# Two chained attentions and a max-of-three feed-forward layer: a new written order for the first two batches, an engine chosen for each copy, and a few idle products

## The chip, the cores and the metric

One core of a Trainium2 chip. The metric is the time of one execution in microseconds as the device measures it. The kernel before took 503.29 us (median of 3 runs, 502.99 to 503.62).

## The reference

Eight batches of 576 rows, eight heads of 64 columns. Keys and values are first packed by 32 learned rows `p`; the queries then attend to the 32 packed rows, which are keys and values at once. The heads side by side (4608 rows x 512) go through a feed-forward layer whose hidden value is the largest of three products.

```
p_packed = sm_attn(p, k, v)                 # softmax(p k^T / 8) v, per batch and head
out      = sm_attn(q, p_packed, p_packed)
x        = out, heads side by side          # 4608 x 512
h        = max(x @ w1, x @ w2, x @ w3)      # 4608 x 768
result   = h @ w_out                        # 4608 x 512
```

## The kernel before

The unit of work is a step: a Python generator that issues a few instructions and yields. Its name is a letter and digits, the first digit being the batch b (0 to 7). The heads of a batch are kept in two groups r = 0, 1, and the 576 rows in two halves of 288.

- `S` scores of `p` against the keys (L209); `A` the largest value, the exponential and the turn by TensorE (L222 to L256), per r; `Z` the inverse of the sum; `V` products with the values (L268); `K` the turn of the packed rows and their copy to `pt` (L283, L285).
- `Q` products of the queries with `pt` (L295), in two halves for batch 0. `B` the softmax over 32 columns, per r, for batch 0 also per half: turn (L318), maximum (L322), subtraction (L324), exponential (L326), sum (L329), inverse (L331, L333), multiplication (L335), turn (L338), and the split into a rounded high part `a2h` and a remainder `a2l` (L122, L127).
- `P` projects: as `x` is a combination of packed rows, each of the six column blocks j of the hidden layer needs `pt` times the weights (L356), scaled and split into `ph` (L365, ScalarE) and `pl` (L367, VectorE).
- `N` the hidden layer (L389), in groups of 6 products of 128x288 (high by high, low by high, high by low, for two r), called mi here; `E` the maximum of three (L399, L403, L405); `H` its split.
- `O` the output product (L434, called mo), `F` its copy and store.
- `C` converts weights, which are stored as 64-bit words: two ScalarE steps (L173, L178), one of VectorE (L184), one of GpSimd (L188). Each j takes three transfers `wi`. `k`, `v`, `q`, `w` are loads, all on SP's queue.

For batches 2 to 7 a table of due times (`STAGES`) and `tick` set the order on TensorE, and the scheduler that of the other engines. For batches 0 and 1, the conversion of all weights and the first part of batch 2, the order on every engine is written by hand: the table `START`, one word per advance of a step. A word ending in v, g or a sends what the advance issues to VectorE, GpSimd or ScalarE, where `on` or `split_hi` asks. Each engine works through its own queue in order.

Buffers that matter: two large PSUM tiles (tag `big`) serve the scores, the turned scores of batches above 0 and the projections; four PSUM banks (tag `moe`) serve the sums of N and O; `ph` and `pl` have three buffers each; q two; four tiles of `stage` hold weights on arrival; SP's loads are written in the order of `START`, and at most eight are under way, since each waits for the landing of the one eight before it.

Of the kernel before, what the change touches and what calls it, by code (L numbers as in the profile page):

```python
# [51 lines left out]
B011 A10 C11 N00 C12 N00 B001v E000 A11 B011g C11 E000 A11 E000 N00 C20 P01 Z11 C20 Z10 A10 P01 N00 w31
C22 A10 P01 C22 N00 A11 E001 C21 N01 E001 C21 A11 E001 N01 E010 C31 V101 w32 C30 q10 E010 C30 C31 q11
w40 H00a N01 V101 w41 H00g K1 P02 E010 K1 C32 C31 N01 P02 C31 N01 P02 E011 C32 N01 w42 E011 Q1 C32 E011
C32 H01a N02 B11 C40 w50 H01g N02 C40 B11 N02 E020 B10 B11g C41 N02 C41 B10 P10 B11 B10v E021 N02 B11
B10 P11 E020 B11 P10 B11 B10 B11g N02 C42 E020 B10 P11 B10 B11 B10g C42 P10 B11 B10 P03 C50 B11g E021
B10 E021 P03 B10v C50 P11 N10 H02a C42 N10 E100 C40 N10 P03 C42 N10 E100 C40 E100 N10 E101 N10 E101 w51
H02g N11 E101 H10a N11 C41 E110 C50 N11 E110 C41 N11 C51 E110 N11 C51 w52 C50 w60 E111 N11 w61 E111 w62
H10g N03 w63 E111 H11a N03 C51 E030 N03 C52 C51 E030 P04 E030 C52 H11g C60 N03 P04 N03 E031 P04 N03 C61
E031 N04 C61 E031 C60 N04 C52 C61 E040 N04 C52 C63 E040 N04 C62 E040 C60 C63 P12 C61 E041 C62 N04 P12  # L60
C60 N04 E041 C61a P12 P05 w64 C60a w65 C61v N12 H03a E041 C60g P05 N12 H04a P05 N12 H03g C64 N12 C64 P13
C63 E120 C62 E121 E120 C62 N12 C65 E120 P13 N12 E121 k20 C63 C65 P13 N05 C62a N05 E121 k21 C63a H04v N05
H12a C63v N05 E050 C62v N05 E051 E050 H12g N05 E050 E051 N13 C65 E051 C65 N13 E130 H05a N13 E130 C65a
H05v N13 E130 C65g N13 E131 N13 C64 O0 E131 C64 E131 O0 H13a O0 v20 C64v v21 C64v O0 q20 q21 H13g O0 O0
F00 O0 F01 O0 O0 O0 F02 O0 O0 O0 F03 O0 O0 O0 F04 O0 O0 P14 F05 O0 P14 O0 P14 O0 O0 F06 O0 O0 N14 F07
N14 E140 N14 E140 P15 E140 N14 P15 N14 P15 E141 N14 E141 N15 E141 H14a N15 E150 H14v N15 E150 N15 E150
# [14 lines left out]
def fused_kernel(ctx: ExitStack, tc: tile.TileContext, kp, qt, va, vb, wi, wo, out):  # L81
# [80 lines left out]
    def convert(j, c):  # L162

        words = staged.pop((j, c)).bitcast(U32).rearrange("p (n two) -> p n two", two=2)
        low, high = words[:, :, 0], words[:, :, 1]
        nc.scalar.activation(  # L173
            out=high.bitcast(F32), in_=high.bitcast(F32), func=AF.Prelu, scale=2.0 ** -111, alpha=-2.0 ** 32,
        )
# [66 lines left out]
    def turn(b, r):  # L242
# [6 lines left out]
        a = a1[b, r][0]  # L249
        for t in range(SF):  # L250
            nc.tensor.transpose(out=tp[:, t * P:(t + 1) * P], in_=a[:, t * P:(t + 1) * P], identity=ident)  # L251
# [4 lines left out]
        nc.scalar.copy(out=at[0:SR, SF, :], in_=pa[0:SR, 0:P])  # L256
# [23 lines left out]
    def packed(b):  # L280

        pt = av.pop((b, 1))[:, 2 * P:3 * P]
        nc.tensor.transpose(out=pt, in_=pp.pop(b).rearrange("p r d -> p (r d)"), identity=ident)  # L283
        yield 1
        nc.scalar.copy(out=pt_sb[b % 2], in_=pt)  # L285
# [64 lines left out]
    def project(b, j):  # L350

        ps = ps_big.tile([P, R, 512], F32, name=f"pw{b}_{j}", tag="big")
        for n in range(4):
            for r in range(R):
                o = slice(64 * r, 64 * r + 64)
                nc.tensor.matmul(  # L356
                    out=ps[NP * n:NP * n + NP, r, 0:NW * P],
                    lhsT=pt_sb[b % 2][o, NP * n:NP * n + NP],
# [6 lines left out]
        nc.scalar.activation(out=hi, in_=ps[:, :, 0:NW * P], func=AF.Copy, scale=2.0 ** -WS)  # L365
        yield 1
        nc.vector.scalar_tensor_tensor(  # L367
            out=lo, in0=ps[:, :, 0:NW * P], scalar=2.0 ** -WS, in1=hi.bitcast(F32), op0=ALU.mult, op1=ALU.subtract,
        )
# [88 lines left out]
    def keep_warm(n):
        t = ps_moe.tile([P, 512], F32, name="idle", tag="moe")
        for _ in range(n):  # L460
            nc.tensor.matmul(out=t[:, 0:P], lhsT=ident, rhs=ident, start=True, stop=True)

# [146 lines left out]
```

## Time and profile before

| | |
|---|---|
| time, median of 3 runs | 503.29 us |
| the profiled execution: time, span | 503.85 us, 502.1 us |
| TensorE busy | 479.2 us, 95% of the span |
| VectorE, ScalarE, GpSimd busy | 237.1, 209.6, 129.5 us |
| mean granted clock of TensorE | 0.983 |
| mean traffic with memory | 102 GB/s of the span |

The span runs from the first to the last instruction; 1.75 us of the time lie outside it. A row of the timeline gives start and duration in us, the engine, the line of the kernel, the tile written and those read, and in brackets the idle time ahead and what ended it. Durations of neighbouring rows overlap by some 0.1 us, as instructions are pipelined: the distance between two starts says what one costs in a full queue.

### The profile page before, as it was taken

How to read it: one execution, taken by the hardware profiler on the slowest of the kernel's cores; microseconds unless marked ns; L12 is line 12 of the kernel's file. 1: busy time of each engine (PE TensorE's matmuls, PEld its weight loads, DVE VectorE, ACT ScalarE, POOL GpSimd, SP SyncE). 2: the span in 40 equal slices, each digit the busy share in tenths (PEclk: the TensorE clock that was granted, in tenths of full speed). 3: DMA queues.
4: the chain of work that ended last, by engine and by line, in shares of the span. 5: the costliest groups of instructions: out<-in, count | busy, mean ns of one | idle time of the engine just before them, and what ended most of it. 6: DMA issues, size and time to landing. Idle time of an engine off the chain costs nothing.

```text
span 502.1 us, 11442 instructions
## 1 busy us (share of the span) xinstructions
PE 479.2 (95%) x4888; PEld 425.9 (85%) x4888; DVE 237.1 (47%) x483; ACT 209.6 (42%) x437; POOL 129.5 (26%) x104
## 2 busy tenths in 40 slices
PE   4569899999999999999999999999999999999997
PEld 2238698998997989988899899989899898999997
DVE  1595947812436548054551537235470536524410
ACT  3776859412325534244342434335341443433321
POOL 0377576510002223212240222201241122302200
PEclk9679899999999999999999999999999999999999
DMA  8957272451262322130321222112331000110001
GB/s 298 407 206 277 70 252 86 153 189 49 89 207 96 106 95 95 72 112 19 116 99 72 106 88 103 48 49 105 95 119 48 25 3 1 47 48 1 1 25 71
DMA packets 17250, 52.11 MB, mean 104 GB/s; under 512 B 1968, under 2 KB 4272, under 8 KB 17200
## 3 DMA queue, kind: packets, MB, share of 16 engines
q1 hardware_dynamic: 17200, 51.39, 29.0%
q8 instruction: 38, 0.62, 0.5%
q14 instruction: 12, 0.10, 0.1%
HBM read 41.94 MB, written 9.44 MB: 102 GB/s over the span
## 4 chain that ended last, share of the span: by engine, by line
PE 87%; DMA 7%; ACT 1%; DVE 1%; POOL 1%; issue 1%; SPq 1%; ACTq 0%; DVEq 0%; POOLq 0%
PE mi L389 44%; PE mo L434 31%; PE pw L356 6%; DMA wi<-in_wi 4%; DMA v<-in_va 2%; PE tp L268 2%; DMA q<-in_qt 2%; PE s L295 1%; PE s L209 1%; PE tp L251 1%; POOL w_sb L188 1%; ACT wi L173 0%; DVE wo_lo L127 0%; PE tp L252 0%; SPq L151 0%
## 5 line engine op out<-in xcount | busy, mean ns | idle before, releaser
L389 PE MATMUL mi<-a2h,ph 128*128 128x288 f32 x576 | 176.6, 307 | 3.6 <-ACT ph L365 2.4
L389 PE MATMUL mi<-a2h,pl 128*128 128x288 f32 x576 | 170.7, 296 | 1.6 <-DVE pl L367 1.6
L389 PE MATMUL mi<-a2l,ph 128*128 128x288 f32 x576 | 170.8, 297 | 0.4 <-POOL a2l L127 0.4
L434 PE MATMUL mo<-h,wo_hi 128*128 128x288 f32 x768 | 156.6, 297 | 0.0
L389 PEld LDWEIGHTS mi<-a2h,ph 128*128 128x128 f32 x576 | 108.8, 189 | 29.1 <-issue 15.4
L434 PEld LDWEIGHTS mo<-h,wo_hi 128*128 128x128 f32 x768 | 124.3, 188 | 2.3 <-issue 1.6
L434 PE MATMUL mo<-h,wo_lo 128*128 128x288 f32 x384 | 113.8, 296 | 0.0
L127 POOL TENSOR_TENSOR h<-hf,h 128x576 fp32r<-128x576 f32 x38 | 54.5, 1435 | 221.5 <-ACT h L122 221.5
L389 PEld LDWEIGHTS mi<-a2h,pl 128*128 128x128 f32 x576 | 109.0, 189 | 1.9 <-DVE pl L367 1.9
L389 PEld LDWEIGHTS mi<-a2l,ph 128*128 128x128 f32 x576 | 108.8, 189 | 0.9 <-POOL a2l L127 0.6
L367 DVE SCALAR_TENSOR_TENSOR pl<-pw,ph 128x768 fp32r<-128x768 f32 x48 | 44.7, 952 | 109.3 <-ACT ph L365 109.3
L399 ACT COPY c<-mi 128x288 f32<-128x288 f32 x96 | 38.2, 398 | 82.6 <-PE mi L389 81.8
L434 PEld LDWEIGHTS mo<-h,wo_lo 128*128 128x128 f32 x384 | 72.3, 188 | 0.2 <-DVE wo_lo L127 0.2
L403 DVE TENSOR_TENSOR c<-mi,c 128x288 f32<-128x288 f32 x96 | 43.5, 453 | 60.8 <-PE mi L389 60.0
L447 ACT ACTIVATE o<-mo 128x288 f32<-128x288 f32 x64 | 26.2, 411 | 99.3 <-PE mo L434 95.1
L405 DVE TENSOR_TENSOR hf<-mi,c 128x288 f32<-128x288 f32 x96 | 43.8, 456 | 25.3 <-PE mi L389 22.5
L122 ACT CAST h<-hf 128x576 fp32r<-128x576 f32 x48 | 32.3, 673 | 48.0 <-DVE hf L405 47.3
L356 PE MATMUL pw<-w_sb,pt 64*32 64x384 f32 x768 | 40.1, 503 | 4.8 <-DVE e L318 2.1
L365 ACT ACTIVATE ph<-pw 128x768 fp32r<-128x768 f32 x48 | 37.0, 808 | 15.1 <-PE pw L356 15.0
L324 POOL TENSOR_TENSOR e<-e,m 128x576 f32<-128x576 f32 (+1 forms) x15 | 15.7, 1063 | 60.6 <-PE mo L434 45.8
L188 POOL TENSOR_TENSOR w_sb<-w_sb,wi 128x512 int32<-128x512 int32 x18 | 24.4, 1364 | 25.1 <-DMA wi<-in_wi 14.8
L356 PEld LDWEIGHTS pw<-w_sb,pt 64*32 64x32 f32 x768 | 11.1, 106 | 17.1 <-issue 13.1
(64 smaller groups left out, 329.5 us busy)
## 6 DMA issues: line engine op xcount, KB each, us to landing
kt<-in_kp SPq DMA_DIRECT2D x16, 640.0 KB, 5.1
wi<-in_wi SPq DMA_DIRECT2D x18, 512.0 KB, 8.5
out_t<-o SPq DMA_DIRECT2D x31, 288.0 KB, 2.1
v<-in_va SPq DMA_DIRECT2D x16, 512.0 KB, 4.5
q<-in_qt SPq DMA_DIRECT2D x14, 576.0 KB, 5.2
wo<-in_wo SPq DMA_DIRECT2D x6, 512.0 KB, 6.8
q<-in_qt SPq DMA_DIRECT2D x4, 288.0 KB, 8.0
v<-in_vb SPq DMA_DIRECT2D x16, 64.0 KB, 4.7
```

The costliest lines, as they stand in the source:

```text
L122: e.copy(out=hi, in_=src)
L127: on(default).tensor_tensor(out=lo, in0=src, in1=hi.bitcast(F32), op=ALU.subtract)
L188: nc.gpsimd.tensor_tensor(out=dst.bitcast(I32), in0=dst.bitcast(I32), in1=up, op=ALU.add)
L356: nc.tensor.matmul(out=ps[NP * n:NP * n + NP, r, 0:NW * P], lhsT=pt_sb[b % 2][o, NP * n:NP * n + NP], rhs=w_sb[o, j, n * NW * P:(n + 1) * ...
L365: nc.scalar.activation(out=hi, in_=ps[:, :, 0:NW * P], func=AF.Copy, scale=2.0 ** -WS)
L367: nc.vector.scalar_tensor_tensor(out=lo, in0=ps[:, :, 0:NW * P], scalar=2.0 ** -WS, in1=hi.bitcast(F32), op0=ALU.mult, op1=ALU.subtract,)
L389: nc.tensor.matmul(out=sums[b, j, hf, x][:, 0:HS], lhsT=w[:, r, x * P:(x + 1) * P], rhs=a[:, c], start=(r == 0 and n == 0), stop=(r == R - ...
L399: nc.scalar.copy(out=c1, in_=sums[b, j, hf, 0][:, 0:HS])
L403: nc.vector.tensor_tensor(out=c1, in0=sums[b, j, hf, 1][:, 0:HS], in1=c1, op=ALU.max)
L405: nc.vector.tensor_tensor(out=hidden[b, j][:, c], in0=sums[b, j, hf, 2][:, 0:HS], in1=c1, op=ALU.max)
L434: nc.tensor.matmul(out=sums[b, m, hf][:, 0:HS], lhsT=w[:, j, x], rhs=a[:, c], start=(j == 0 and i == 0), stop=(j == NJ - 1 and i == 2),)
L447: nc.scalar.activation(out=o[:, c], in_=sums.pop((b, m, hf))[:, 0:HS], func=AF.Copy, scale=2.0 ** -WS)
```

## The change

`START` is written anew: 575 words in place of 568. The set of steps is the same, but for five words `I`, and for two advances more of step `P00`. With it:

- `copy` takes the place of `split_hi`, and now serves the copies of the turned scores (L255, L256), of `pt` (L285) and of the first of three sums (L399) too, so that a word's ending moves them to VectorE; the addition of 1e-9 (L331) and the output copy (L447) can go there as well.
- `I` no longer issues products at once: it sets a count, and the next step of `S`, `A`, `Q`, `P` or `N` that begins issues as many products of the identity with itself into its own PSUM tile first (`rouse`). The count is the word's first digit: `I10` gives one. In all there are seven: one ahead of S0, of the first turn, of Q0 and of P00, and three ahead of the first mi.
- `P00` writes two of the four `moe` banks, one per r, and splits them apart; before it took a `big` tile and did both at once.

The table itself shows nothing to a reader; its first two lines before and now are:

```diff
-k00 k01 v00 v01 w00 q000 q010 w01 w02 q001 q011 w10 w11 w12 S0 w20 w21 w22 k10 A00 k11 w30 A01 A00 A01
-A00 Z00 C00 Z01 A01 A00 A01 V00 C01 V01 V00 C01 v10 C02 V01 C01 v11 K0 C02 C01 K0 C00 Q0 C02 Q0 C00 B000
+k00 k01 I10 S0 w11 C11 C11 v01 w00 w02 v00 A01 A00 w01 A01 A00 q010 I10 A01 A00 A01v Z00 Z01 C11 A00v
+C00 C02 C00 C00 C02 C01 V01 C11 C00 q000 V00 V00 V01 K0 q001 q011 C01 w12 C02 C01 K0a I1 Q0 B000 Q0 B010
...
+    def copy(out, src, default="a"):
         e = on(default)
         if e is nc.scalar:
-            e.copy(out=hi, in_=src)
-        else:
-            e.tensor_copy(out=hi, in_=src)
+            e.copy(out=out, in_=src)
+        else:
+            e.tensor_copy(out=out, in_=src)
...
+    idle = [0]
+
+    def rouse(ps):
+
+        for _ in range(idle[0]):
+            nc.tensor.matmul(out=ps[:, 0:P], lhsT=ident, rhs=ident, start=True, stop=True)
+        idle[0] = 0
...
     def project(b, j):
 
-        ps = ps_big.tile([P, R, 512], F32, name=f"pw{b}_{j}", tag="big")
+        parts = [slice(0, R)]
+        if b == 0 and j == 0:
+
+            parts = [slice(r, r + 1) for r in range(R)]
+            ps = [ps_moe.tile([P, 512], F32, name=f"pw{b}_{j}_{r}", tag="moe") for r in range(R)]
+            src = [x[:, 0:NW * P].unsqueeze(1) for x in ps]
+        else:
+            x = ps_big.tile([P, R, 512], F32, name=f"pw{b}_{j}", tag="big")
+            ps, src = [x[:, r] for r in range(R)], [x[:, :, 0:NW * P]]
+        rouse(ps[0])
...
             if kind == "I":
-                keep_warm(x[0])
+                idle[0] = x[0]
```

SP's queue at the program's start. `wi0_1` is the second transfer of the weights of j = 0, `v1` the values of head group 1 of batch 0 (a transfer of 4 KB rows and a small one), `kt` keys, `q` half of the queries. Before:

```order
L144 DMA kt0_81<-in_kp 128x1280
L144 DMA kt1_83<-in_kp 128x1280
L150 DMA v0_85<-in_va 128x1024
L151 DMA v0_85<-in_vb 64x256
L150 DMA v1_88<-in_va 128x1024
L151 DMA v1_88<-in_vb 64x256
L138 DMA wi0_0_91<-in_wi 128x512
L159 DMA q0_93<-in_qt 128x2x288
L159 DMA q1_95<-in_qt 128x2x288
L138 DMA wi0_1_97<-in_wi 128x512
```

Now:

```order
L154 DMA kt0_81<-in_kp 128x1280
L154 DMA kt1_83<-in_kp 128x1280
L148 DMA wi1_1_104<-in_wi 128x512
L160 DMA v1_108<-in_va 128x1024
L161 DMA v1_108<-in_vb 64x256
L148 DMA wi0_0_111<-in_wi 128x512
L148 DMA wi0_2_113<-in_wi 128x512
L160 DMA v0_115<-in_va 128x1024
L161 DMA v0_115<-in_vb 64x256
L148 DMA wi0_1_126<-in_wi 128x512
```

Three transfers of weights, one of them for j = 1, moved ahead of the second part of the values; the queries now follow the tenth load.

VectorE's queue from the first turn of batch 0's scores on. `s2_0_0` is the PSUM tile of r = 0, `s2_0_1` that of r = 1, `m2` maxima, `z2` sums; each turn takes one half of 288. Before:

```order
L318 STREAM_TRANSPOSE e0_0_258<-s2_0_0_238 128x288
L322 TENSOR_REDUCE m2_0_0_0_262<-e0_0_258 128x9
L324 TENSOR_TENSOR e0_0_258<-e0_0_258,m2_0_0_0_262 128x288
L318 STREAM_TRANSPOSE e0_0_258<-s2_0_0_238 128x288
L318 STREAM_TRANSPOSE e0_1_270<-s2_0_1_239 128x288
L329 TENSOR_REDUCE z2_0_0_0_273<-e0_0_258 128x9
L322 TENSOR_REDUCE m2_0_1_0_275<-e0_1_270 128x9
L333 RECIPROCAL z2_0_0_0_273<-z2_0_0_0_273 128x9
L335 TENSOR_TENSOR e0_0_258<-e0_0_258,z2_0_0_0_273 128x288
L338 STREAM_TRANSPOSE et0_0_293<-e0_0_258 128x288
```

Now:

```order
L331 STREAM_TRANSPOSE e0_0_237<-s2_0_0_226 128x288
L331 STREAM_TRANSPOSE e0_1_247<-s2_0_1_227 128x288
L335 TENSOR_REDUCE m2_0_1_0_249<-e0_1_247 128x9
L335 TENSOR_REDUCE m2_0_0_0_251<-e0_0_237 128x9
L331 STREAM_TRANSPOSE e0_0_237<-s2_0_0_226 128x288
L331 STREAM_TRANSPOSE e0_1_247<-s2_0_1_227 128x288
L335 TENSOR_REDUCE m2_0_0_288_261<-e0_0_237 128x9
L335 TENSOR_REDUCE m2_0_1_288_265<-e0_1_247 128x9
L337 TENSOR_TENSOR e0_0_237<-e0_0_237,m2_0_0_288_261 128x288
```

All four turns and maxima now stand ahead of the first sum. The first turn is written between the two halves of Q0, and the second half of Q0 waits for it, as both touch the same tile. Nine more instructions stand between this piece and the turn `et0_0` of the first half.

TensorE's queue around the projection P03. `pw0_3` is its result, `pw1_1` that of batch 1's second, `mi0_2_1_2` the third sum of the second half of batch 0's j = 2. Before:

```order
L389 MATMUL mi0_2_1_1_696<-a2l0_1_376,ph0_2_587 128x288
L356 MATMUL pw1_1_706<-w_sb_72,pt1_76 32x384 x8
L389 MATMUL mi0_2_1_2_725<-a2h0_0_297,ph0_2_587 128x288
L389 MATMUL mi0_2_1_2_725<-a2h0_0_297,pl0_2_588 128x288
L389 MATMUL mi0_2_1_2_725<-a2l0_0_304,ph0_2_587 128x288
L389 MATMUL mi0_2_1_2_725<-a2h0_1_374,ph0_2_587 128x288
L389 MATMUL mi0_2_1_2_725<-a2h0_1_374,pl0_2_588 128x288
L389 MATMUL mi0_2_1_2_725<-a2l0_1_376,ph0_2_587 128x288
L356 MATMUL pw0_3_748<-w_sb_72,pt0_75 32x384 x8
L389 MATMUL mi1_0_0_0_771<-a2h1_0_761,ph1_0_718 128x288
```

Now:

```order
L417 MATMUL mi0_2_1_0_693<-a2h0_1_370,pl0_2_634 128x288
L417 MATMUL mi0_2_1_0_693<-a2l0_1_373,ph0_2_633 128x288
L381 MATMUL pw0_3_709<-w_sb_72,pt0_75 32x384 x8
L381 MATMUL pw1_1_737<-w_sb_72,pt1_76 32x384 x8
L417 MATMUL mi0_2_1_1_747<-a2h0_0_336,ph0_2_633 128x288
L417 MATMUL mi0_2_1_1_747<-a2h0_0_336,pl0_2_634 128x288
```

Before, P10, P11 and P03 stand with 6 mi between each two, and batch 1's mi begin behind P03. Now P02 and P10 stand together, 36 mi follow, then P03 and P11 together, then 48 mi more of batch 0 ahead of batch 1's first. Two more moves are told of below: batch 1's scores S1 stand ahead of the first mi and no longer behind 6 of them, and P01 stands behind 6 mi and no longer behind 24. From batch 2's first mi on, the instructions of TensorE stand as before.

More of the change, by code (lines that the diff above doesn't have):

```diff
@@ L52 @@
[L52 to L66, printed above, removed]
@@ new lines @@
+B010 B000 B001 C02 C01 B000g B010g C12 B011 C12 B001 B000 B010 B011 B001v k11 C12 w10 k10 B001 I1 P00
+B000 P00 B010 B000a B011g B001 B011 B010a C12 w22 P00 B000 B010 B000v B001a B001 C10 C10 B000 S1 w21
+B010g B001v C10 B000a B000g B001 B011 P00 C22 B011a A10 B010 A10 B001a I3 N00 C10 B011 B010v B011v B010g
+P01 P00 B011 C21 N00 P01 A11 A11 C22 N00 B011v A10 P01 A11 E000v w31 v11 v10 w20 E000 C21 C31 B001g E000
+B011g C22 A11v A10a N00 N00 V101 C31 C20 C20 N00 C22 C21 Z11 Z10 V101 C21 q11 K1 C20 E001v N01 q10 w30
@@ new lines @@
+K1a Q1 E001 E001 w32 C20 H00v C31 N01 H00g E010a B10 C31 N01 C30 w42 N01 P02 w41 E011a B11 B10 C32 P10
+E010 w60 P02 B10g C32 E010 N01 B11 B11g N01 C30 B10 B11 P02 C32 C30 E011 N02 N02 E020a N02 P10 B11 E011
+B11a N02 C32 P10 B10 H01a C30 E020 P03 B10a B10 E020 B11 H01g B10g P03 E021v w40 w62 w61 w51 P11 P03 N02
+N02 N03 B11g E021 B10 E021 E030a N03 H02a C41 N03 B11 B10v N03 E030 B10g B11a N03 E030 C42 C40 C42 N03
+C40 C41 E031v B11v N10 E031 N10 E031 H02g C40 C41 P11 E100a C42 N10 E100 N10 E100 P11 N10 C41 C62 H03a
@@ new lines @@
+E101a C42 C40 N10 w63 w50 C60 N11 C63 C62 P12 P04 C60 q20 C61 C60 E101 E101 E110v P12 C63 C60 H03v C51
+P04 N11 E110 w65 w52 N11 P12 C62 N11 C51 N11 E110 E111v E111 N11 E111 C50 N12 P04 N12 C62 E120v C50 H10a
+C60a N12 N12 C62a H10v E120 C61 E121v E120 N12 N04 N12 N04 E121 C62g P13 C52 C60v C50 C52 C51 C51 H11a
+C52 P14 C61 H11g C65 E040a P13 C50 E121 P13 E040 N04 N04 N13 E041v E040 E130v H12a P14 H12g N13 N04 k20
+E130 C65 C63 E041 N13 N04 N13 C52 E130 P14 P05 C61 E041 P05 C61a E131a P15 H04v w64 P05 N13 N13 C63 N05
@@ new lines @@
+N05 E131 E131 E050a C61g P15 H04g N05 N14 N14 E050 C63a C64 H13v N05 H13g k21 E050 E140a C63v E140 P15
+N14 N14 N05 C65 C65 E051v N05 E140 N14 E141a C64 N14 C65a E051 C64 E051 E141 H05a C64 C65v E141 C64v O0
+C64v O0 O0 N15 H05v O0 O0 E150v v20 F00a N15 O0 S2 O0 O0 O0 F01a A21 A20 N15 O0 O0 E150 E150 F02v N15 O0
+F03v N15 O0 A20 E151a A21 O0 O0 O0 O0 O0 E151 O0 F04a O0 O0 N15 F06a q21 v21 O0 A20 Z20 E151 Z21 A21 O0
+O0 H14a A21a F05v O1 O1 H15a A20v O1 H14g V201 O1 H15v F07v V201 K2 K2v O1 O1 O1 O1 F10a O1 O1 Q2 v30
@@ L71 @@
+B21 B20 O1 B20 B21 O1 B20v q31 O1 B20 O1 O1 P20 F11v P20 O1 B21v F12v O1 v31 O1 B20 O1 F13a B21 O1 F14a
+B20v B20 q30 P20 k31 B21 F15a B21a O1 B20g O1 B21 B20 B21g O1 B20a k30 B21 B21a F16a B20v B21v O1 F17a
 """
@@ L190, in convert @@
             yield 2
-            split_hi(wo_hi[:, c], dst)
+            copy(wo_hi[:, c], dst)
             yield 1
@@ L249, in turn @@
         a = a1[b, r][0]
+        rouse(tp)
         for t in range(SF):
@@ L254, in turn @@
         at = pool.tile([P, SF + 1, P], F32, name=f"a1t{b}_{r}", tag="a1t", bufs=2)
-        nc.scalar.copy(out=at[:, 0:SF, :], in_=tp.rearrange("p (t x) -> p t x", x=P))
-        nc.scalar.copy(out=at[0:SR, SF, :], in_=pa[0:SR, 0:P])
+        copy(at[:, 0:SF, :], tp.rearrange("p (t x) -> p t x", x=P))
+        copy(at[0:SR, SF, :], pa[0:SR, 0:P])
         a1t[b, r] = at
@@ L284, in packed @@
         yield 1
-        nc.scalar.copy(out=pt_sb[b % 2], in_=pt)
+        copy(pt_sb[b % 2], pt)
     def queries(b):
@@ L330, in attend @@
         yield 0
-        nc.scalar.activation(out=z, in_=z, func=AF.Copy, bias=1e-9)
+        if on("a") is nc.scalar:
+            nc.scalar.activation(out=z, in_=z, func=AF.Copy, bias=1e-9)
+        else:
+            nc.vector.tensor_scalar_add(out=z, in0=z, scalar1=1e-9)
         yield 0
@@ L340, in attend @@
         hi = buffer("a2h", "a2h", 4, F32R)
-        split_hi(hi, et)
+        copy(hi, et)
         yield 0
@@ L356, in project @@
                 nc.tensor.matmul(
-                    out=ps[NP * n:NP * n + NP, r, 0:NW * P],
+                    out=ps[r][NP * n:NP * n + NP, 0:NW * P],
                     lhsT=pt_sb[b % 2][o, NP * n:NP * n + NP],
@@ L364, in project @@
         lo = pool.tile([P, R, NW * P], F32R, name=f"pl{b}_{j}", tag="pl", bufs=3)
[L365 to L369, printed above, removed]
-        pw[b, j] = (hi, lo)
+        pw[b, j] = (hi, lo)
+        for r, x in zip(parts, src):
+            nc.scalar.activation(out=hi[:, r], in_=x, func=AF.Copy, scale=2.0 ** -WS)
+            yield 1
+            nc.vector.scalar_tensor_tensor(
+                out=lo[:, r], in0=x, scalar=2.0 ** -WS, in1=hi[:, r].bitcast(F32), op0=ALU.mult, op1=ALU.subtract,
+            )
+            yield 1
     hid, sums, hidden = {}, {}, {}
@@ L383, in layer_in @@
                     sums[b, j, hf, x] = ps_moe.tile([P, 512], F32, name=f"mi{b}_{j}_{hf}_{x}", tag="moe")
+                rouse(sums[b, j, hf, i])
                 steps = [((2 * i + x) % 3, (2 * i + x) // 3) for x in range(2)] if first else [(i, 0), (i, 1)]
@@ L398, in maximum @@
         c1 = pool.tile([P, HS], F32, name=f"c1_{b}_{j}_{hf}", tag="c1", bufs=2)
-        nc.scalar.copy(out=c1, in_=sums[b, j, hf, 0][:, 0:HS])
+        copy(c1, sums[b, j, hf, 0][:, 0:HS])
         yield 0
@@ L413, in halves @@
             hl = pool.tile([P, 2, S], F32R, name=f"h{b}_{j}", tag="h", bufs=NJ + 1)
-        split_hi(hl[:, 0], h)
+        copy(hl[:, 0], h)
         yield 0
@@ L446, in finish @@
         o = outs[b, m]
-        nc.scalar.activation(out=o[:, c], in_=sums.pop((b, m, hf))[:, 0:HS], func=AF.Copy, scale=2.0 ** -WS)
+        ps = sums.pop((b, m, hf))[:, 0:HS]
+        if on("a") is nc.scalar:
+            nc.scalar.activation(out=o[:, c], in_=ps, func=AF.Copy, scale=2.0 ** -WS)
+        else:
+            nc.vector.tensor_scalar(out=o[:, c], in0=ps, scalar1=2.0 ** -WS, scalar2=None, op0=ALU.mult)
         if b == B - 1 and m == NM - 1:
@@ L456, in weigh_and_turn @@
         yield from turn(b, r)
[L458 to L461, printed above, removed]
     stages = {
```

10 lines of the change are left out of this document (2 added, 8 removed).

## The prediction

> **What bounds the kernel now.** I read the busy shares first, then the list of what TensorE waited for, then the windows.
>
> ```profile
> PE 479.2 (95%) x4888; PEld 425.9 (85%) x4888; DVE 237.1 (47%) x483; ACT 209.6 (42%) x437; POOL 129.5 (26%) x104
> ...
> PE mi L389 <- DVE c L403: 0.6, 1, 0.6
> ```
>
> TensorE is the bound: busy for 95% of the span, and of its waits on others (us in total, times, longest) the one shown, 0.6 at 93 us, is the only one behind 60 us. What can be won lies ahead of that. The windows show where (stretch, its length, busy us of each engine, granted clock, DMA share, GB/s):
>
> ```profile
> 0.00:11.72 11.72, 4.61 (x38) 2.08 (x39) 2.36 (x8) 3.15 (x6) 0.70 (x6) 1.00 0.86 294
> 0.00:14.40 14.40, 7.03 (x90) 3.82 (x93) 2.36 (x8) 5.08 (x11) 0.70 (x6) 1.00 0.89 313
> 17.30:31.00 13.70, 7.44 (x86) 3.11 (x86) 11.69 (x28) 11.11 (x26) 6.45 (x9) 0.50 1.02 399
> 31.00:58.33 27.33, 23.69 (x313) 17.69 (x305) 21.24 (x46) 19.75 (x41) 20.09 (x17) 1.00 0.50 171
> 42.30:58.40 16.10, 14.37 (x230) 10.63 (x237) 12.32 (x25) 12.87 (x25) 10.27 (x9) 1.00 0.62 220
> 54.92:58.33 3.41, 1.68 (x30) 1.04 (x22) 3.28 (x7) 3.41 (x7) 2.60 (x3) 1.00 0.00 0
> 58.33:61.65 3.32, 3.32 (x23) 1.86 (x8) 3.22 (x7) 2.84 (x5) 1.26 (x2) 0.50 0.00 0
> 61.65:500.00 438.35, 436.59 (x4368) 398.76 (x4367) 197.14 (x394) 168.35 (x352) 99.84 (x73) 1.00 0.24 82
> ```
>
> From 61.65 us on TensorE idles 1.8 us in 438, at full clock; what the order there costs can hardly fall. Ahead of it, the clock is half from 17.3 to 31.0 and again from 58.33 to 61.65. These spells, 13.7 and 3.3 us, and the 27.33 between them are 4, 1 and 8 times about 3.41 us: the clock is set anew on a grid of that step. The grid step 54.92 to 58.33, with TensorE busy for 1.68, was followed by half clock.
>
> TensorE's timeline of the start (start, duration; half clock shows in durations also where the column says 1.00, since four turns take 1.09 at 10 us and 0.60 at 40 us):
>
> ```profile
> 10.45 1.09 PE L251 MATMUL tp<-ident,a 128*128 128x128 f32 x4 [2.07 <-ACT a L227]
> ...
> 13.07 2.12 PE L268 MATMUL pa<-v,a1t 128*32 128x64 f32 x80 [0.26 <-ACT a1t L256]
> 15.69 0.33 PE L283 MATMUL pa<-ident,pp 128*128 128x128 f32 x1 [0.49 <-DVE pp L278]
> 17.48 2.18 PE L295 MATMUL s<-q,pt 64*32 64x288 f32 x32 [1.46 <-ACT pt L285]
> 21.77 1.53 PE L356 MATMUL pw<-w_sb,pt 64*32 64x384 f32 x16 [2.11 <-DVE e L318]
> ...
> 27.88 0.61 PE L389 MATMUL mi<-a2h,pl 128*128 128x288 f32 x1 [1.56 <-DVE pl L367]
> ...
> 28.76 0.44 PE L389 MATMUL mi<-a2h,pl 128*128 128x288 f32 x1
> 29.00 0.44 PE L389 MATMUL mi<-a2l,ph 128*128 128x288 f32 x1
> 29.37 1.98 PE L209 MATMUL s<-kt 64*32 64x288 f32 x32
> ...
> 40.15 0.60 PE L251 MATMUL tp<-ident,a 128*128 128x128 f32 x4
> ...
> 42.36 1.46 PE L268 MATMUL tp<-v,a1t 128*32 128x64 f32 x80
> 43.75 0.40 PE L389 MATMUL mi<-a2h,ph 128*128 128x288 f32 x1
> ...
> 44.64 0.27 PE L283 MATMUL tp<-ident,pp 128*128 128x128 f32 x1
> 44.84 0.88 PE L356 MATMUL pw<-w_sb,pt 64*32 64x384 f32 x16
> 45.65 0.40 PE L389 MATMUL mi<-a2h,ph 128*128 128x288 f32 x1
> ...
> 48.24 1.20 PE L295 MATMUL s<-q,pt 64*32 64x288 f32 x32
> 49.37 0.40 PE L389 MATMUL mi<-a2h,ph 128*128 128x288 f32 x1
> ...
> 58.13 1.42 PE L356 MATMUL pw<-w_sb,pt 64*32 64x384 f32 x16 [1.74 <-DVE pl L367]
> 59.48 0.61 PE L389 MATMUL mi<-a2h,ph 128*128 128x288 f32 x1
> ```
>
> TensorE runs short of work until 27.88, and once more at 56.4, where P03, the third projection within a few us, waits for VectorE to empty one of two large tiles. From distances of starts I take, at full clock: an mi 0.138 (36 in 4.97, below), V 1.39, K 0.20, a projection 0.81, Q 1.13, five turns 0.46 (40.15 to the next mi at 40.61). At half clock: an mi 0.24, a projection 1.35.
>
> ```profile
> 157.22 4.97 PE mi L389 x36
> ```
>
> **The change part by part.** I follow the new order along the path to the first mi, then to a point X at which both orders have done the same: 60 mi, P00, P01, P02, P10, S1, V1, K1, Q1. Before, 54 of these mi and all but Q1 and P10 are done at 45.65, so X is worth 45.65 + 6 x 0.138 + 1.13 + 0.81 = 48.4.
>
> *The values.* V0 needs the second part of the values, now behind three transfers of weights: it is complete after 4.06 MB (keys 1.31, three weights 1.57, values 1.18). Before, the first weights are complete after 3.01 MB, and ScalarE takes them at 11.72:
>
> ```profile
> 11.72 0.67 ACT L173 ACTIVATE wi<-wi 128x512 f32<-128x512 f32 x1 [0.57 <-DMA wi<-in_wi]
> ...
> 17.18 0.24 ACT L285 COPY pt<-pa 128x128 f32<-128x128 f32 x1
> ```
>
> By then 11.72 x 294 = 3.45 MB have moved, 0.44 more than its own; 4.06 + 0.44 = 4.50 MB are moved at 14.4. So V0 starts at 14.4, not 13.07, and ends at 16.5. Two scalings on VectorE (0.3 each), K 0.33 and the copy of `pt` 0.24 bring Q0 to 17.8: 0.3 later. The copies of the turned scores, now on VectorE, cost nothing: the values are later than they. Nor does the one product ahead of each step, since it stands in a wait.
>
> *The softmax of batch 0.* The first half of Q0 (1.09) ends at 18.9; its second half now waits for the first turn (0.48 and a hop), and ends at 20.5, against 19.66. Then VectorE has a full queue up to `et0_0`:
>
> ```profile
> 20.28 0.45 DVE L322 TENSOR_REDUCE m<-e 128x9 f32<-128x288 f32 x1
> 20.77 0.46 DVE L324 TENSOR_TENSOR e<-e,m 128x288 f32<-128x288 f32 x1
> 21.14 0.84 DVE L318 STREAM_TRANSPOSE e<-s 128x288 f32<-128x288 f32 x2
> ...
> 23.07 0.90 DVE L335 TENSOR_TENSOR e<-e,z 128x288 f32<-128x288 f32 x1
> ...
> 22.98 0.67 POOL L324 TENSOR_TENSOR e<-e,m 128x288 f32<-128x288 f32 x1 [2.56 <-DVE m L322]
> ```
>
> Three turns at 0.42, seven reductions at 0.36, two steps of two inputs, one conversion 0.42, half a `pl` 0.48, three inverses at 0.15 and the turn 0.48. A step of two inputs took 0.46 alone and 0.90 beside GpSimd's row at 22.98; I take 0.90 for both, since GpSimd has three subtractions and a conversion there now. Sum 1.26 + 2.52 + 1.80 + 0.42 + 0.48 + 0.45 + 0.48 = 7.4 (6.5 without GpSimd), so `et0_0` at 28.1, its rounding on ScalarE 0.43, the first mi at 28.7. By the Trainium skill, page "SBUF — State Buffer", section "Who interferes with whom", GpSimd and a VectorE step with two inputs there exclude each other for a whole instruction; by that the two would cost up to 0.67 more each, 0.46 in all above mine. P00 no longer waits for the turns (2.11), but that is no gain: its `ph` is ready some 3 us ahead of `a2h`.
>
> *P01.* Six mi at half clock end at 30.1. P01 needs a large tile, both of which hold S1, and so waits for VectorE's maximum of S1 (0.71, behind five other rows from 28.1: 30.6) and ScalarE's exponential (0.73): 31.4. TensorE is thus busy for about 1.5 us of the grid step 27.6 to 31.0. That is below the 1.68 after which the clock fell, so I keep half clock until 34.4, 3.4 later than before. (The skill, page "TensorE: Matmul & The Clock Gate", Part 1, has half clock come after an idle window of about 3.4 us; here a wait of 1.74 was enough, so the measurement decides.) From 31.4: P01 to 32.75, 7 mi at 0.24 to 34.4, then 47 mi (6.5), ten turns (0.9), V1 1.39, K1 0.20, Q1 1.13 and two projections (1.6) make 11.7: X at 46.2 with 0.1 for hops. Gain 48.4 - 46.2 = 2.2. It comes from S1 and Q1, Q1 ahead of the mi that it feeds and S1 in the shade of a wait.
>
> *P03.* P02 and P10 now take the two tiles together, and 36 mi (5.0 us) pass until P03 and P11 need them; VectorE has to read two of 0.95 in that time, among others. The wait of 1.74 goes, and with it the spell of half clock, half of 3.32: together 3.4. The 0.6 at 93 us stands in an order that is gone: 0.6.
>
> *What comes in.* VectorE now also rounds and copies. From Q1's end (42.1) to the end of batch 1's `a2l` I count 4 turns (0.42), 6 steps of 576 columns, 3 `pl`, 10 maxima and 8 others. The groups give the durations (us of all, mean ns of one, idle ahead), of which 0.08 overlap:
> ```profile
> L367 DVE SCALAR_TENSOR_TENSOR pl<-pw,ph 128x768 fp32r<-128x768 f32 x48 | 44.7, 952 | 109.3 <-ACT ph L365 109.3
> L405 DVE TENSOR_TENSOR hf<-mi,c 128x288 f32<-128x288 f32 x96 | 43.8, 456 | 25.3 <-PE mi L389 22.5
> ...
> L329 DVE TENSOR_REDUCE z<-e 128x18 f32<-128x576 f32 x14 | 10.4, 746 | 1.1 <-ACT e L326 0.7
> ```
>
> With 0.67, 0.87, 0.37 and, for the others, 0.42 as the conversion (roundings and copies on VectorE have no row; their ends are 0.37 and 0.87) that is 1.7 + 4.0 + 2.6 + 3.7 + 3.4 = 15.4 us without a gap, against 12.32 busy in 16.10 before. TensorE has 102 mi and 4 projections up to there, 17.3 us; the margin is 1.9. Its price lies between nothing and 3.4 (such a wait with a spell of half clock, as at 56.4); I take 1.3, between the waits of 0.6 and 1.74 shown, without a spell. Weights arrive in another order; costed at nothing, since the DMA share is 0.50 from 31 to 58 us, and those of j = 5 are not needed before about 80.
>
> Sum: 2.2 + 3.4 + 0.6 - 1.3 = 4.9. Against the profiled execution 503.85 that is 498.95; the median of the runs lies 0.56 below it, so 498.4.
>
> **The rivals.**
>
> *VectorE becomes the bound* between 42 and 58 us. GpSimd was busy for 10.27 of these 16.1 us; if VectorE's steps within SBUF each wait for it, VectorE falls behind by a part of that. At half, 5.1 - 1.9 leaves a wait of 3.2, plus 1.66 for half clock: the gain is 6.2 - 4.9 = 1.3, time 502.0. At three quarters, 5.8 + 1.66 = 7.5 eats all: 504.6, slower. It decides from 6.4 us of such waits. For it: 0.90 against 0.46 above. Against it: sums, maxima and turns, most of the string, show no such stretch (0.45 at 20.28, 0.84 for two at 21.14). 0.12 for the first, 0.06 for the second, 0.06 for what lies between (503.3, no change).
>
> *The clock rises a step later*, at 37.8, because P01 or the mi behind it come late: 1.7 more, 500.1. For it: the grid's phase need not be the same in every execution. 0.18.
>
> *The idle products hold the clock up.* The skill's page on TensorE (same part) says that a busy window releases it, and idle products are busy time. Here it would spare Q0 and P00 1.8 and the mi up to 34.4 about 0.7: 495.9. Against it: seven products of 0.27 (row at 44.64) are 1.9 us over 28. 0.06.
>
> **How the numbers follow.** The likeliest case, 498.4, has 0.52; its own range is 497.0 to 499.9. Over 0.2% (1.0 us, about what a measurement of this kernel tells from no change) faster end the main case, the later clock, the idle products and most of VectorE's milder case: 0.86; within it 0.08; slower 0.06. The range 496.0 to 502.2 leaves out VectorE's two dearer cases (0.12) and half of the idle products', and holds the ends of the unknown costs (0 to 3.4 for the new wait, 1.7 for the clock).
>
> **What would show it.** Right: V0 near 14.4, Q0 near 17.8, first mi at 28 to 29, clock full from about 34, no wait of 1 us or more at P03, no second spell of half clock. Wrong: a wait of over 1.7 us between 42 and 62 us with half clock behind it, or V0's start beyond 15.5 us.

## The result and the profile after

The kernel after takes 495.36 us (median of 4 runs, 495.02 to 497.80), the kernel before beside it 503.46 (4 runs, 502.99 to 503.87): a ratio of 0.985, 95% interval 0.9817 to 0.9883. The forecast was 498.4 with a range of 496.0 to 502.2. The direction was right; the gain, 8.1 us, is larger than the 4.9 forecast, and the time lies outside the range. The profiled execution took 495.23 us with a span of 493.4, against 503.85 and 502.1 before.

The page's busy shares and, in the second fence, the whole list of TensorE's waits in the kernel after (us in total, times, longest):

```profile
PE 478.6 (97%) x4902; PEld 428.5 (87%) x4902; DVE 247.1 (50%) x517; ACT 196.4 (40%) x404; POOL 129.5 (26%) x105
```
```profile
PE s L220 <- DMA kt<-in_kp: 5.1, 3, 2.7
PE s L136 <- POOL ident masks.py:199: 1.4, 1, 1.4
PE tp L263 <- ACT a L238: 1.3, 1, 1.3
PE pw L381 <- ACT a L238: 1.2, 1, 1.2
PE pa L280 <- DMA v<-in_va: 1.0, 1, 1.0
PE s L308 <- DVE e L331: 0.6, 1, 0.6
PE pa L295 <- DVE pp L290: 0.6, 1, 0.6
```

All of these stand ahead of 31.4 us; the waits for `pl` and for `c` that stood at 56.4 and 93 us before are gone, and the list has none in their place (a delay of 0.2 at 58.73, told of below, is not in it). TensorE's busy time is the same as before within 0.6 us, although seven idle products came in: other work became cheaper, as told of below.

TensorE's timeline of the start (start, duration, and in brackets the idle time ahead and its releaser):

```profile
13.86 2.83 PE L280 MATMUL pa<-v,a1t 128*32 128x64 f32 x80 [0.96 <-DMA v<-in_va]
...
18.15 1.21 PE L308 MATMUL s<-q,pt 64*32 64x288 f32 x16
...
21.86 1.53 PE L381 MATMUL pw<-w_sb,pt 64*32 64x384 f32 x16
25.47 2.29 PE L220 MATMUL s<-kt 64*32 64x288 f32 x32 [2.08 <-DMA kt<-in_kp]
27.69 1.65 PE L136 MATMUL mi<-ident 128*128 128x128 f32 x6
28.99 0.49 PE L417 MATMUL mi<-a2h,ph 128*128 128x288 f32 x1
29.32 0.29 PE L417 MATMUL mi<-a2h,pl 128*128 128x288 f32 x1
...
31.34 0.88 PE L381 MATMUL pw<-w_sb,pt 64*32 64x384 f32 x16 [1.16 <-ACT a L238]
...
43.85 1.52 PE L381 MATMUL pw<-w_sb,pt 64*32 64x384 f32 x32
```

V0 at 13.86 (forecast 14.4), Q0 at 18.15 (17.8), the first mi at 28.99 (28.7), P01 at 31.34 (31.4): the path was followed closely. What differs is the clock. S1 stands directly ahead of the idle products and those directly ahead of the mi, so that TensorE has work without a gap from 25.47 to 30.2; three idle products are six rows and take 1.30 us at half clock. From 29.32 on the mi start 0.13 apart, and P01 takes 0.88: full clock five microseconds ahead of the 34.4 that the prediction kept. The clock rises at about 29.2, so the grid does not lie here as the prediction had it (27.6, 31.0, 34.4). So the point X, forecast at 46.2, is at 45.30.

Two rows that mark how far each kernel is at batch 2's first mi, behind which both have the same order: before and, in the second fence, after.

```profile
157.15 0.40 PE L389 MATMUL mi<-a2h,ph 128*128 128x288 f32 x1
```
```profile
148.12 0.40 PE L417 MATMUL mi<-a2h,ph 128*128 128x288 f32 x1
```

So 9.03 us are won by there, and the output products of the last batch still start 9.03 us earlier (470.40 against 479.43); 0.3 go again behind TensorE's last product, which leaves 8.7 in the span.

### The profile page after: what moved, and what is told of

It is laid out like the page before. It is cut to its first block, busy times and chain, and to the rows that moved or that the text cites. A ratio compares the mean times of both kernels' runs of the same rounds, so it can differ in the third digit from the quotient of the medians.

```text
span 493.4 us, 11471 instructions
## 1 busy us (share of the span) xinstructions
PE 478.6 (97%) x4902; PEld 428.5 (87%) x4902; DVE 247.1 (50%) x517; ACT 196.4 (40%) x404; POOL 129.5 (26%) x105
## 4 chain that ended last, share of the span: by engine, by line
PE 94%; DVE 2%; DMA 2%; SPq 1%; issue 0%; ACT 0%; ACTq 0%; DVEq 0%
PE mi L417 48%; PE mo L462 31%; PE pw L381 7%; PE s L308 2%; PE tp L280 2%; DMA v<-in_va 2%; PE s L220 1%; PE tp L263 1%; PE pa L280 1%; DVE e L331 0%; PE tp L264 0%; SPq L148 0%; DVE z L342 0%; DVE m L335 0%; DVE w_sb L194 0%
## 5 line engine op out<-in xcount | busy, mean ns | idle before, releaser
L394 DVE SCALAR_TENSOR_TENSOR pl<-pw,ph 128x768 fp32r<-128x768 f32 (+1 forms) x49 | 44.9, 935 | 92.9 <-ACT ph L392 92.8
L124 ACT COPY c<-mi 128x288 f32<-128x288 f32 x84 | 33.5, 399 | 84.4 <-PE mi L417 80.7
L477 ACT ACTIVATE o<-mo 128x288 f32<-128x288 f32 x58 | 23.8, 411 | 97.0 <-PE mo L462 92.4
L124 ACT CAST h<-hf 128x576 fp32r<-128x576 f32 x45 | 30.3, 673 | 39.2 <-DVE hf L433 37.8
L392 ACT ACTIVATE ph<-pw 128x768 fp32r<-128x768 f32 (+1 forms) x49 | 37.3, 795 | 17.5 <-PE pw L381 17.4
L381 PE MATMUL pw<-w_sb,pt 64*32 64x384 f32 x768 | 37.7, 496 | 1.2 <-ACT a L238 1.2
L129 POOL TENSOR_TENSOR a2l<-et,a2h 128x576 fp32r<-128x576 f32 (+1 forms) x15 | 18.9, 1274 | 28.2 <-ACT a2h L124 25.4
```

Of the source, the lines that this page charges most:

```text
L124: e.copy(out=out, in_=src)
L381: nc.tensor.matmul(out=ps[r][NP * n:NP * n + NP, 0:NW * P], lhsT=pt_sb[b % 2][o, NP * n:NP * n + NP], rhs=w_sb[o, j, n * NW * P:(n + 1) * ...
L392: nc.scalar.activation(out=hi[:, r], in_=x, func=AF.Copy, scale=2.0 ** -WS)
L394: nc.vector.scalar_tensor_tensor(out=lo[:, r], in0=x, scalar=2.0 ** -WS, in1=hi[:, r].bitcast(F32), op0=ALU.mult, op1=ALU.subtract,)
L477: nc.scalar.activation(out=o[:, c], in_=ps, func=AF.Copy, scale=2.0 ** -WS)
```

## The experiments

Times are medians on one chip for each group, beside the kernel before there: 504.13 us for the first group (no idle products, an idle block ahead of P03, P00 in one tile, 39 idle products), 504.50 for the second (split pairs, copies on ScalarE, P01 later, an idle block ahead of N00), 504.48 for the third (first pairs apart, and the kernels after and with 39 idle products again). The kernel after took 495.49 in the third group (494.69 to 498.18). It did not run in the first two groups; differences from it are taken from this 495.49, and the kernel before, which ran in all three, differs by 0.4 between them.

**Without the idle products.** The words `I10`, `I10`, `I1`, `I1` and `I3` are struck from the written order.

> The new order with no idle products. Clock theory: the three ahead of the first mi, with S1, fill a step of the clock's grid, so that full clock comes at 29 us and not a step (3.4 us) later; without them the first six mi, P01 and some mi run at half clock, 1.2 to 1.9 us more: 496.6 to 497.3. Rival: S1 and the mi raise the clock by themselves, or the grid happened to lie well: within 0.3 us of 495.4.

496.97 us (496.49 to 497.06), ratio 0.9862 (0.9839 to 0.9885). The idle products are worth 1.5 us here, and the theory is right. TensorE's timeline:

```profile
28.41 0.61 PE L417 MATMUL mi<-a2h,ph 128*128 128x288 f32 x1 [0.51 <-ACT a2h L124]
...
31.23 1.54 PE L381 MATMUL pw<-w_sb,pt 64*32 64x384 f32 x16 [0.61 <-ACT a L238]
...
34.55 0.36 PE L417 MATMUL mi<-a2h,pl 128*128 128x288 f32 x1
34.74 0.30 PE L417 MATMUL mi<-a2l,ph 128*128 128x288 f32 x1
```

The first mi is even 0.6 earlier, but the clock stays half until 34.7 and P01 takes 1.54: this kernel does what was forecast of the kernel after (full from 34.4, X at 46.2; here X is at 46.5).

**More idle products.** 39 in place of seven, some of them ahead of the values too, and all in places where TensorE waits:

```diff
-k00 k01 I10 S0 ... q010 I10 A01 A00 ... C01 V01 ... K0a I1 Q0 ... B001 I1 P00 ... B000 S1 ... B001a I3 N00
+k00 k01 I7 S0 ... q010 I4 A01 A00 ... C01 I9 V01 ... K0a I3 Q0 ... B001 I4 P00 ... B000 I6 S1 ... B001a I6 N00
...
+        rouse(av[b, rs[0]][:, 2 * P:3 * P])
```

> The new order with 39 idle products in place of seven, also ahead of V0 and S1. Clock theory: full clock from 9 to 12 us on, V0 in 1.4 and not 2.9, Q0 in 1.2 and not 2.4, so the softmax of batch 0 and the first mi come 1.5 to 2 us earlier: 493.4 to 494.0. Rival (transfers set the pace: values at 13.9, S1's keys at 25.5, weights of j = 1): at most 0.4 us less, 495.0.

494.41 us (494.37 to 494.45), ratio 0.9813 (0.9791 to 0.9835): faster than both kernels, and between the two expectations. The timeline:

```profile
13.45 1.73 PE L258 MATMUL pa<-v,a1t 128*32 128x64 f32 x80
...
21.54 0.88 PE L359 MATMUL pw<-w_sb,pt 64*32 64x384 f32 x16
22.48 1.58 PE L113 MATMUL s<-ident 128*128 128x128 f32 x12
25.55 1.30 PE L197 MATMUL s<-kt 64*32 64x288 f32 x32 [1.50 <-DMA kt<-in_kp]
26.79 1.60 PE L113 MATMUL mi<-ident 128*128 128x128 f32 x12
28.15 0.38 PE L395 MATMUL mi<-a2h,ph 128*128 128x288 f32 x1
...
30.59 0.88 PE L359 MATMUL pw<-w_sb,pt 64*32 64x384 f32 x16 [1.14 <-ACT a L215]
```

V0 takes 1.73 for 2.83, P00 0.88 for 1.53, S1 1.30 for 2.29; yet the first mi comes only 0.8 earlier and P01 0.75, since keys and softmax come when they come. Of the 2.7 us that TensorE saves in these three, 0.75 reach batch 2's first mi (147.37).

**The kernels after and with 39 idle products once more, on one chip.**

> The kernel after, unchanged, beside the others on one chip: 0.983 to 0.985 of the kernel before.

> The kernel with 39 idle products, unchanged, beside the kernel after on one chip: 0.9 to 1.1 us below it if its gain is that of the chip's clock at the start and not of another chip.

495.49 us (494.69 to 498.18), ratio 0.9837 (0.981 to 0.9864), and 494.36 (494.16 to 494.67), ratio 0.9803 (0.9783 to 0.9823): 1.1 apart, as expected. Of all ten runs of the kernel after, three took 497.67 to 498.18 and seven 494.69 to 495.54; the nine with 39 idle products lie within 0.5 us. The profiled one of the kernel after here is one of the three:

```profile
25.96 1.32 PE L220 MATMUL s<-kt 64*32 64x288 f32 x32 [1.92 <-DVE w_sb L194]
27.21 1.40 PE L136 MATMUL mi<-ident 128*128 128x128 f32 x6
29.15 0.61 PE L417 MATMUL mi<-a2h,ph 128*128 128x288 f32 x1 [0.54 <-ACT a2h L124]
...
31.98 1.53 PE L381 MATMUL pw<-w_sb,pt 64*32 64x384 f32 x16 [0.61 <-ACT a L238]
...
37.33 0.42 PE L264 MATMUL tp<-ident,a 128*64 128x128 f32 x1
37.55 0.71 PE L263 MATMUL tp<-ident,a 128*128 128x128 f32 x4
```

Here the clock was full at S1 (1.32), earlier than in the other execution, fell again behind the wait of 1.92, and stayed half until about 37.6: X is at 48.3, 3.0 later, and the time 2.7 over the median. Seven idle products are just enough in most executions and not in all. This is the rival of the later clock, in three runs of ten by their times; only this one of the three has a profile. P01 came 0.6 later than in the other execution, so it is the place of the grid, and not a late P01, that made the difference: here a step of it ended at about 24.0, ahead of the wait, and not at 29.2.

**An idle block in the kernel before, ahead of its first mi.**

```diff
-P00 B011 B001 B010 B011 N00 C22
+P00 B011 B001 B010 B011 I9 N00 C22
```

> The kernel before, with nine idle products ahead of its first mi (in a bank of their own): TensorE waited there 2.41 us for ScalarE's ph and then 1.56 for VectorE's pl, at half clock until 31. Nine take some 3.9 us at half clock. The clock should be full a grid step earlier, from about 27.6. Theory (a full clock pays only where TensorE has work ready; in the old order two waits stand right behind, of 0.60 and 0.40 us for the softmax at 32 to 33.5, and take it back): 0 to 0.4 below the kernel before. Rival (the idle products are worth their 1.6 us by themselves, whatever the order): 1.2 to 1.8 below.

503.88 us (502.76 to 505.07, 12 runs), ratio 0.9999 (0.9986 to 1.0012): nothing. The timeline:

```profile
23.56 2.97 PE L461 MATMUL idle<-ident 128*128 128x128 f32 x18
26.29 0.38 PE L389 MATMUL mi<-a2h,ph 128*128 128x288 f32 x1
27.99 0.40 PE L389 MATMUL mi<-a2h,pl 128*128 128x288 f32 x1 [1.33 <-DVE pl L367]
...
32.15 0.40 PE L389 MATMUL mi<-a2h,ph 128*128 128x288 f32 x1 [1.21 <-ACT a2h L122]
```

The clock is full from within the idle block on (from about 25.0, 6 us ahead of the 31.0 before); the mi run at full speed into the wait for `a2h`, which grows from 0.60 to 1.21. The theory is right: ahead of the first mi, idle products pay only together with the order that has the softmax ready behind them.

**An idle block in the kernel before, ahead of P03.** Seven idle products in a bank of their own: `project` issues them ahead of its own products when it is P03's turn; the table stays.

> The kernel before, with seven idle products of 128x128 in a bank of their own ahead of P03, in its wait of 1.74 us. Clock theory (a grid step about half idle is followed by half clock, and any product counts as work): the spell of half clock from 58.3 to 61.7 goes, 1.5 to 1.7 us less than before: 501.7 to 501.9. Rival (the spell has another cause, or idle products do not count): no change, 503.2 to 503.6.

503.07 us (502.91 to 503.74), ratio 0.9986 (0.9973 to 0.9998): less than the theory had it. P03 takes 0.88 instead of 1.42 and no half clock follows, but of the 1.66 us that the spell cost two new waits (0.41 for `a2h`, 0.33 for `a2l`) take 0.74 back. So the spell is real, and in the old order it is worth 0.8 at batch 2's first mi (156.35), not 1.66. The rest of the 3.4 would need P03's wait itself gone.

**P00 in one large tile.** The change's small tiles for P00 are undone (`if b == 0 and j == 0:` made false); the rest stays.

> The new order with P00 in one large tile, split in one piece, as before. As the prediction had it, P00's banks are no gain, since its high part is ready early: within 0.4 us of 495.4. Rival: S1 needs both large tiles, so it then waits until VectorE has read P00 (about 28 us, not 25.5), and the first mi, the maximum of S1 and P01 come later: 2 to 3.5 us more, 497.4 to 498.9.

496.02 us (495.65 to 496.14), ratio 0.9843 (0.982 to 0.9865): 0.5 more than the kernel after, between the two expectations. P00 waits 2.0 for VectorE's turns again, S1 behind it cannot have its second large tile until VectorE has read P00 (a wait of 0.5), and the first mi comes at 30.47 instead of 28.99; but the wait ahead of P01 shrinks, so that X is 0.9 later. The prediction costed this part at no gain.

**The copies back on ScalarE.** The suffix `v` is struck from the 23 words of kinds A, K, E and F that have it (`E000v` becomes `E000`).

> The kernel after, with the 23 copies (turned scores, pt, c, the scaled output) that the change puts on VectorE put back on ScalarE; order and idle products stay. Theory (ScalarE and VectorE both have slack there, so the choice is worth little): 495.0 to 496.0. Rival (the choice is what keeps TensorE without a wait behind 32 us): waits of 0.5 to 1 us come back in the first two batches, 496.3 to 498.5.

497.20 us (496.96 to 498.06), ratio 0.9866 (0.9846 to 0.9886): 1.7 more than the kernel after. The two rows below are waits for ScalarE that the kernel after does not have:

```profile
37.78 1.46 PE L280 MATMUL tp<-v,a1t 128*32 128x64 f32 x80 [0.34 <-ACT a1t L124]
...
60.58 0.40 PE L417 MATMUL mi<-a2h,ph 128*128 128x288 f32 x1 [0.52 <-ACT c L124]
```

With 0.15 for GpSimd's weights at a projection at 66.6 they are 1.0 of the 1.7. Another 0.5 was lost ahead of 35.6 us, where the mi behind the turns start (35.09 in the kernel after), and may be scatter of the start. So the choice of engine is worth about 1 us: the rival, in the lower half of its range.

**Pairs split in the later batches.** One number in each of three entries of the plan; TensorE's work and everything else stay.

```diff
-STAGES = "P1:0 P2:0 ... P3:12 P4:12 ... P5:26 P6:26 ..."
+STAGES = "P1:0 P2:1 ... P3:12 P4:13 ... P5:26 P6:27 ..."
```

> The kernel after, with the two projections of each pair one step of the grid (three mi) apart in batches 2 to 7: 18 pairs become 36 single visits; nothing else differs. Theory of the passage (each change of TensorE between the 64x32 products of a projection and the 128x128 products of mi costs some 0.1 us each way: in the trace of the kernel before a single visit takes about 1.0 us from the last mi to the first behind it, a pair 1.7): 18 times 0.3, about 5 us more than the kernel after, 499 to 501.5. Rival (a passage is free, and the 2 us that batch 1 gained beyond the waits come from elsewhere): within 0.6 of the kernel after, 494.9 to 496.

501.81 us (501.19 to 502.13), ratio 0.9954 (0.9936 to 0.9971): 6.3 more than the kernel after, without a new entry in TensorE's list of waits. From the first output product of batch 2 to that of batch 3, the windows (stretch, its length, busy us of each engine) give for the kernel after

```profile
185.54:243.71 58.17, 58.17 (x613) 52.84 (x612) 26.60 (x56) 22.16 (x47) 12.16 (x10) 1.00 0.24 83
```

and with the pairs split

```profile
186.79:246.05 59.26, 59.26 (x613) 52.57 (x612) 26.62 (x56) 22.51 (x47) 12.17 (x10) 1.00 0.24 82
```

The same 613 rows keep TensorE busy for the whole of 58.17 us in the one and 59.26 in the other: 1.09 us for three pairs. A projection by itself costs 0.36 us more than one behind another, and it counts as busy time. Over the whole run the traces show 40 visits of projections from 40 us on, against 24: 16 pairs came apart and not the 18 expected, since batch 2's first three projections make a pair and a single there as in the kernel after, and the last batch issues no projection for a next one. 16 times 0.36 are 5.8; the spans profiled differ by 6.3, of which 0.34 stand ahead of the first pair.

**Pairs split in the first batches.** In the written order the second word of each of the five pairs is moved behind the next six mi (`P11 P03 N02` becomes `P03 N02 P11`).

> The kernel after, with the five pairs of projections that its written order makes in batches 0 and 1 (P02+P10, P03+P11, P12+P04, P13+P14, P05+P15) taken apart: six mi stand between the two of each pair, as they stood in the kernel before. Theory (the pairs are worth 0.36 us each, which is what 18 split pairs of the later batches cost: the time of a batch rose by 1.08 us with three pairs split): 1.5 to 2.2 us more than the kernel after, with no new wait of TensorE. Rival (the batch-1 gain beyond the waits comes from somewhere else in the order): within 0.5 of the kernel after.

496.70 us (496.20 to 497.22), ratio 0.9851 (0.9828 to 0.9874): 1.2 more than the kernel after beside it, under the 1.5 to 2.2 expected. The execution profiled had P01 0.4 earlier; from the first pair (43.42 here, 43.85 after) to the first output product (97.87, 96.98) it took 1.3 more, 0.26 a pair, or 0.30 if the 0.2 that the kernel after waits at 58.73 and this one doesn't are set against it; no new wait came. The theory stands, a little smaller. The second pair, together in the kernel after:

```profile
50.05 0.29 PE L417 MATMUL mi<-a2l,ph 128*128 128x288 f32 x1
50.27 1.52 PE L381 MATMUL pw<-w_sb,pt 64*32 64x384 f32 x32
51.72 0.40 PE L417 MATMUL mi<-a2h,ph 128*128 128x288 f32 x1
51.96 0.30 PE L417 MATMUL mi<-a2h,pl 128*128 128x288 f32 x1
```

and split:

```profile
49.96 0.29 PE L416 MATMUL mi<-a2l,ph 128*128 128x288 f32 x1
50.19 0.88 PE L380 MATMUL pw<-w_sb,pt 64*32 64x384 f32 x16
50.99 0.40 PE L416 MATMUL mi<-a2h,ph 128*128 128x288 f32 x1
51.23 0.29 PE L416 MATMUL mi<-a2h,pl 128*128 128x288 f32 x1
...
51.98 0.88 PE L380 MATMUL pw<-w_sb,pt 64*32 64x384 f32 x16
52.79 0.40 PE L416 MATMUL mi<-a2h,ph 128*128 128x288 f32 x1
```

The price is read from the starts: mi follow each other by 0.13, the projection follows an mi by 0.22 to 0.23, the second mi behind it follows the first by 0.24, and a pair pays this once: in one piece 50.05 to 51.72 is 1.67, each half by itself 1.03, 0.39 more for the two, of which 0.13 is an mi's own. With the slower second mi 0.11 more: 0.37. The Trainium skill, page "TensorEngine Tiling (Array Packing)", section "Key Properties", has it that a change of the tiling mode drains TensorE; the projections are 64x32 and the mi 128x128, and the trace agrees in so far as each change costs time. It shows the price, not a drain itself.

**P01 later.** In the kernel with 39 idle products the second six mi stand ahead of P01, and the second half of P00's `pl` ahead of the maximum of S1 on VectorE:

```diff
-C22 B011a A10 ... B010g P01 P00 B011 C21 N00 P01 A11
+C22 B011a P00 A10 ... B010g B011 C21 N00 P01 P01 A11
```

> The kernel with 39 idle products, changed further: the second six mi of the first sum are put ahead of P01, and the second half of P00's low part ahead of the maximum of S1 on VectorE that they need it for. In the kernel with 39 idle products TensorE waited 1.14 us for P01 with twelve mi of that sum still to do. Theory (any work moved into a wait ahead of 32 us is won in full, less what VectorE's later maximum costs, up to 0.5): 493.5 to 494.0. Rival (the wait only moves, because VectorE's string sets the pace here): 494.3 to 495.

494.92 us (494.64 to 495.35), ratio 0.9818 (0.98 to 0.9837): no gain, 0.5 more. The rival is right: the wait of 1.14 for P01 goes, and 0.18 for `a2h`, 0.43 for `a2l` and 0.70 for ScalarE's `a` come. All three are made from what VectorE puts out, so its string sets the pace up to 33 us.

## Why the prediction was wrong

- *The start.* V0, Q0, the first mi and P01 were forecast within 0.6 us, VectorE's work up to `et0_0` too; its turn ends at 28.0 (forecast 28.1). Right, for timing, but in part by luck. The second half of Q0 ended at 21.2 and not at 20.5, and VectorE's string behind it took 6.8 us and not 7.4: its two steps of two inputs took 0.45 and 0.46 (0.90 each was forecast, as beside GpSimd), its conversion 0.89 (0.42). The two errors cancel. And P00's small tiles were costed at no gain; without them X is 0.9 later, since S1 then waits for P00's large tile.

```profile
24.06 0.45 DVE L337 TENSOR_TENSOR e<-e,m 128x288 f32<-128x288 f32 x1
24.43 0.89 DVE L194 TENSOR_SCALAR w_sb<-wi 128x512 uint32<-128x512 uint32 x1
...
27.02 0.46 DVE L351 TENSOR_TENSOR e<-e,z 128x288 f32<-128x288 f32 x1
...
27.52 0.47 DVE L354 STREAM_TRANSPOSE et<-e 128x288 f32<-128x288 f32 x1
```

- *The clock.* "so I keep half clock until 34.4" failed. I compared the 1.5 us that TensorE would be busy between 27.6 and 31.0 with the 1.68 behind which the clock had once fallen, on a grid that I had taken over from the execution before. I had left out of it S1, which waits for its keys until 25.47 and then runs at half clock, and the idle products behind it, which I put at 0.27 each, the full-clock price; they take 0.43. Together they are a stretch of work without a gap from 25.47 to 30.2, and the clock rose inside it, on a grid that lay otherwise than forecast. That the grid lay so was luck: on the forecast's grid neither the step to 27.6 nor that to 31.0 is full in these rows (2.1 and 2.6 us of 3.4). The rival to which I gave 0.06 is what happened in seven runs of ten, by their times; its 495.9 came from another sum, though: Q0 and P00 were not spared (1.21 twice and 1.53, half clock), the passage and the waits below made up for it. Size: 1.5 us by the kernel without the idle products, 1.2 of it at X.
- *The projections' passages.* The term "a projection 0.81" was mis-sized. From one projection's first product to the next mi it is 0.81, but a visit costs 0.36 more when it stands alone. Behind X, up to batch 2's first mi, the kernel before makes nine single visits and one pair, the kernel after five pairs and one single: four visits less, 4 x 0.36 = 1.4 us, which the prediction counts at nothing; one pair more lies ahead of X. Both experiments on pairs bear it out (0.36, and 0.26 to 0.30). So "what the order there costs can hardly fall", said of the time from 61.65 us on because TensorE was busy there, failed too: three of the four pairs lie there, and what they save was busy time.
- *The new waits.* "I take 1.3" failed: 0.2 came (at 58.73, where VectorE's `a2l` took 1.83 beside GpSimd). VectorE is nearly full there, as counted (14.97 us busy of the 16.10 from 42.3 to 58.4, below; my sum was 15.4), but the margin of 1.9 us held, and the most likely price of a wait that a margin covers was nothing.

```profile
42.30:58.40 16.10, 16.10 (x163) 13.85 (x162) 14.97 (x30) 11.28 (x22) 13.47 (x11) 1.00 0.73 261
```

- *P03.* The wait and the spell are gone, as forecast; 3.4 was read from the rows and is not measured by itself. 0.6 at 93 us: gone, as forecast.
- *The copies.* They were costed as part of VectorE's load only; that they relieve ScalarE of about 1 us of waits is not in the prediction. It is not one more term of the sum, since the prediction had no such waits in the first place.

- *The other rivals.* VectorE did not become the bound: TensorE was busy for all of the 16.10 us of that row. The later clock, given 0.18 and a price of 1.7, is seen in three runs of ten by their times, where it costs 2.2 to 2.7.

The sum as measured, at batch 2's first mi: X 3.5 (the kernel before at X is 45.65 + 0.80 for six mi + 1.32 for Q1 with the changes of shape around it, 48.02 to 49.61 less two mi, + 1.00 for a single visit = 48.8, an estimate; after 45.30), P03 3.4, 0.6, pairs behind X 1.4, less 0.2: 8.7 of the 9.03. Of the 4.1 by which the gain was under-forecast that places 1.3 in X, 1.1 in the waits, 1.4 in the passages; 0.3 stays unplaced.

## What to carry to other kernels

Work out the clock from the longest stretch in which TensorE has any work without a gap, at the durations of the clock that it has then, and not from the busy share of one window on a grid taken from another execution. A stretch of twice 3.41 us holds a whole step of the grid wherever that lies; the 4.7 us here (25.47 to 30.2) hold one only in some executions (an estimate from these rows). A few idle products that close the last gap can decide it, and enough of them to decide it in every execution are worth more than just enough. But a faster clock ahead of a wait for another engine buys nothing: look first whether the operands behind it are ready. And count changes between products of different array shapes as an operation with a price of its own, since it counts as busy time and no list of waits shows it.
